# The seven-product down matmul in tile 1 as well, its weight sums made during tile 0, and one copy moved to ScalarE in the last two tiles

## The chip, the core and the metric

The kernel runs on one core of a Trainium2 chip. The core has a matrix engine (TensorE, "PE" in the profile), a vector engine (VectorE, "DVE"), a scalar engine (ScalarE, "ACT"), GpSimd ("POOL") and SyncE ("SP"), which here only starts transfers. Each engine works through its own queue strictly in order; between engines there are only semaphores. The metric is the time on the device in microseconds, median of several executions.

## The reference

Two stages follow each other. The first is attention over pooled keys: `k` and `v` (batch 8, heads 8, sequence 576, head size 64) are averaged over groups of 8 tokens, which leaves 72 keys for each head; `q` attends to these with a softmax. The second is a feed-forward layer over the 4608 tokens of 512 features that result:

```python
k_p = k.reshape(B, H, Sp, pool, D).mean(axis=3)
v_p = v.reshape(B, H, Sp, pool, D).mean(axis=3)
scores = scale * np.matmul(q, k_p.transpose(0, 1, 3, 2))
attn = softmax(scores)
x = concat_heads(np.matmul(attn, v_p))
h = x @ w_in                        # 4608x512 @ 512x2048
g = h * np.cos(h)
out = g @ w_out                     # 4608x2048 @ 2048x512
```

## The kernel before

The 4608 tokens are nine tiles of 512, numbered t = 0 to 8; the eight batches of 576 tokens are numbered b. While the feed-forward layer of tile t runs, the attention of batch t + 1 is woven between its matmuls. The order of instructions is written out by hand: each engine's queue holds its instructions in the order in which the program text issues them.

**A tile.** The up part computes `h` in eight pairs of 128 features, 64 matmuls of 512 columns in all (`up_mm`). A pair is written to one of four places in PSUM: `banks[0]` to `banks[2]`, each two banks wide, or the two `obanks`. `up_bank` gives the rotation, and from tile `FIRST` on it is banks 0, 2, 1, obanks, 0, 2, 1, 0. For each pair ScalarE makes the cosine (as a sine with a shifted argument) and VectorE multiplies it with the PSUM values into `g_sb` (`up_g`). A place can be written again only when that multiplication has read it. The down part multiplies `g` with `w_out`. Its outputs are in the `obanks` and leave through VectorE copies and SP transfers.

**Two forms of the down part.** Tiles below `FIRST` (0 and 1 before the change) use the plain one: 64 matmuls of 512 columns, with the attention's steps inserted at given positions of the loop by a list `fill`. Tiles from `FIRST` on use `down_products`: the 2x2 blocks of `g` (features by tokens) and of `w_out` are combined as in Winograd's form of Strassen's method, which needs seven products of blocks in place of eight: 7 x 16 matmuls of 256 columns. For this it needs sums of blocks:

- of the weights, once: `w2`, `w3`, `w4`, made by `put_weights`, and the second column block of the first two weight tiles, replaced in place by a difference in `put_first_weights`. Each has two halves i = 0, 1. `put_weights(0)` is done by GpSimd at the end of tile 0's program text; `put_weights(1)` by VectorE during tile 1's up part; `put_first_weights` by VectorE after tile 1's down part. Each is one operation of 128x1024 bf16, with both inputs in SBUF.
- of `g`, in every tile: `put_g12` (two operations), `put_g3` and `put_g4`, by VectorE, for the first half after the fourth, fifth and sixth up pair, and for the second half after the first products.

The results of the seven products lie in two PSUM places, called A and Bb, and are read out between products by the list `reads`. The first read copies the first product to `p1_sb` by VectorE (`each`, with no other operand). The third product overwrites A and so must wait for that copy. In tiles 1 to 6 attention steps lie between the products (scores after the first, values of one unit after the second, third and fourth); tile 7 has only the rest of the last batch; tile 8 has none, and there A and Bb are spread over separate banks (`apart`).

**Around the change.** GpSimd starts the loads of `k`, `q`, `v` for the batch after next, then (in tile 0) makes `put_weights(0)`, and then pools `k` and `v` by additions (`pool_add`, lines 151 to 159). SP's queue holds the output transfers and the two transposes (`q_transpose`, `k_transpose`), issued during the up part of tiles 1 to 6. At the end of tile 0's down part VectorE has, in this order, the multiplications of the values of batch 1 and the copies of the last two output blocks.

Of the kernel before, what the change touches and what calls it, by code (L numbers as in the profile page):

```python
# [20 lines left out]
def kernel(  # L21
# [9 lines left out]
    nc = tc.nc  # L31
# [11 lines left out]


    ORDER = (0, 2, 4, 6, 1, 3, 5, 7, 8)
    FIRST = 2

    SEG = ((0, 256), (256, 256), (512, 64))
    REST = (SEG[2], (0, H))
# [324 lines left out]
    def down_products(t):  # L374

        def of(w, m=0):
            return lambda fc: w[fc // 4][:, fc % 4, m * HM:(m + 1) * HM]

        def part(x):
            return lambda fc, p: x[:, fc, p * 128:(p + 1) * 128]  # L380

        apart = t == NT - 1
        if apart:
            A, Bb = [[x[:, 0:HM] for x in two] for two in (obanks, (banks[1][:, 0, :], banks[2][:, 0, :]))]
        else:
            A, Bb = [[obanks[i][:, p * HM:(p + 1) * HM] for p in range(2)] for i in (1, 0)]
        products = [
            (A, True, part(g_part(0, 0, 0, HF)), of(w_out_sb[0:2])),
            (Bb, True, part(g_part(1, 0, 0, HF)), of(w_out_sb[2:4])),
            (A, True, part(g2), of(w2)),  # L390
            (Bb, True, part(g1), of(w_out_sb[0:2], 1)),
            (A, False, part(g3), of(w3)),
            (Bb, False, part(g4), of(w_out_sb[2:4], 1)),
            (A, False, part(g_part(1, 1, 0, HF)), of(w4)),
        ]
        mms = []
        for n, (bank, first, g, w) in enumerate(products):
            order = [(fc, p) for fc in range(HF) for p in range(2)]
            if apart and n == 6:
                order.sort(key=lambda x: x[1])  # L400
            for fc, p in order:
                mms.append(lambda bank=bank, first=first, g=g, w=w, fc=fc, p=p: nc.tensor.matmul(  # L402
                    bank[p], lhsT=g(fc, p), rhs=w(fc),
                    start=(first and fc == 0 and (apart or p == 0)), stop=(fc == HF - 1 and (apart or p == 1)),
                    skip_group_check=not first))

        p1, v16, q15 = [msb.tile([128, 2, HM], FP32, name=n, tag=n, bufs=1) for n in ("p1_sb", "v_sb", "q_sb")]
        o1, o2 = [msb.tile([128, 2, d_model], FP32, name="o_two", tag="o_two", bufs=3) for _ in range(2)]
        m1, m2 = slice(0, HM), slice(HM, d_model)

        def each(out, bank, other=None, m=slice(0, HM), tk=None):

            for p in range(2) if apart else (slice(0, 2),):
                ps = bank[p] if apart else obanks[1 if bank is A else 0].rearrange("p (a m) -> p a m", a=2)
                if other is None:
                    nc.vector.tensor_copy(out=out[:, p, m], in_=ps)  # L416
                else:
                    nc.vector.tensor_tensor(out=out[:, p, m], in0=ps, in1=other[:, p], op=ADD)  # L418
                if apart and tk is not None:
                    rows_out(t, tk, out, (p,), m, (nc.sync, nc.scalar))  # L420

        reads = [
            lambda: each(p1, A),
            lambda: each(o1, Bb, p1, m1, 0),
            lambda: each(v16, A, p1),
            lambda: each(q15, Bb, p1),
            lambda: each(o2, A, q15, m2, 1),
            lambda: (each(o1, Bb, v16, m2, 0), apart or rows_out(t, 0, o1)),
            lambda: (each(o2, A, p1, m1, 1), apart or rows_out(t, 1, o2)),
        ]  # L430
        return [mms[i * 2 * HF:(i + 1) * 2 * HF] for i in range(7)], reads
# [99 lines left out]
    for t in range(NT):  # L531
# [5 lines left out]
        for n, fp in enumerate(up_order(t)):  # L537
            up_mm(t, fp, 2 if n < 2 else 0)
            between = ()
            if t == 0:  # L540
                if fp == 4:
                    puts = pool_k_mm(1, obanks[0], 0, 2), pool_k_mm(1, obanks[1], 2, 4)
                elif fp in (5, 6):
                    g0 = 9 * (fp - 5)
                    puts = q_transpose_mm(1, obanks[0], g0, g0 + 5), q_transpose_mm(1, obanks[1], g0 + 5, g0 + 9)
                if fp in (4, 5, 6):
                    puts[0](vec)
                    between = ((puts[1], act),)
            up_g(t, fp, between)
            if t >= FIRST and 3 <= n < 6:  # L550
                (put_g12, put_g3, put_g4)[n - 3](0)
            if t == 1 and 3 <= n < 6:
                put_weights(1, nc.vector, n - 3)
            if 0 < t and b < B:
                if n == 0:
                    q_transpose(b)
                elif n == 2:
                    k_transpose(b)
# [18 lines left out]
        if t == 0:  # L577
            fill[1:] = [(2, S_(0, 0)), (8, lambda: pool_v_mm(1, banks[1])), (8, lambda: values(t, REST, banks[2])),
                        (11, S_(1, 0)), (13, V_(0, 1)), (18, S_(2, 2)), (21, V_(1, 0, later)), (26, S_(3, 1)),
                        (32, lambda: later.pop()()), (32, V_(2, 2)), (40, V_(3, 0))]  # L580
        elif t < FIRST:
            us = BY_TOKENS

            def scores_of(*parts):

                def go():
                    for f in scores_mm, scores_exp:
                        for b_, u, bank in parts:
                            f(b_, u, banks[bank])
                return go  # L590

            fill = [(4, scores_of((b, us[0], 2), (b, us[1], 0))), (14, V_(0, 1, later)), (16, lambda: later.pop()()),
                    (19, V_(1, 2)), (35, scores_of((b, us[2], 0), (b, us[3], 1), (t, REST, 2))),
                    (38, V_(2, 0)), (43, lambda: values(t, REST, banks[1])), (46, V_(3, 2))]
        if t < FIRST:
            fi = 0
            for n, (ms, fc) in enumerate(mms):
                while fi < len(fill) and fill[fi][0] <= n:
                    fill[fi][1]()
                    fi += 1  # L600
                down_mm(obanks[ms % 2], ms, fc)
                if fc == FFCH - 1:
                    down_out(t, ms, obanks[ms % 2])
            if t + 1 == FIRST:
                for i in range(2):
                    put_first_weights(i)
        else:
            products, reads = down_products(t)

            def product(i, j=0, k=2 * HF):  # L610
                for mm in products[i][j:k]:
                    mm()

            us = BY_TOKENS
            later = []

            u0, u1, u2, u3 = [(b, us[i], banks[j]) for i, j in enumerate((2, 1, 0, 1))]
            ur = (t, REST, banks[2])

            def scores_of(*parts):  # L620
                for part in parts:
                    scores_mm(*part)
                for part in parts:
                    scores_exp(*part)

            def muls():
                while later:
                    later.pop(0)()

            steady, rest = b < B, t < B  # L630
            if rest:
                exp_tables()
            product(0)
            if steady:
                scores_of(u0, u1, u2)
            elif rest:
                scores_of(ur)
            product(1)
            put_g12(1)
            reads[0]()  # L640
            put_g3(1)
            reads[1]()
            put_g4(1)
            if steady:
                values(*u0, later)
            product(2)
            reads[2]()
            muls()
            if steady:
                values(*u1, later)  # L650
            product(3)
            reads[3]()
            muls()
            if steady:
                values(*u2, later)
            product(4)
            reads[4]()
            muls()
            if steady:
                scores_of(ur, u3)  # L660
            product(5, 0, 4)
            if rest:
                values(*ur, later)
            product(5, 4, 12)
            muls()
            if steady:
                values(*u3, later)
            product(5, 12)
            reads[5]()
            muls()  # L670
            product(6)
            reads[6]()
# [5 lines left out]
        if b + 1 < B:  # L678
# [2 lines left out]
            load_kv(b + 1, "v", v)  # L681
            if t == 0:
                put_weights(0, nc.gpsimd)
            pool_add(b + 1, "k")
            pool_add(b + 1, "v")
# [28 lines left out]
```

The softmax here doesn't subtract the row's maximum and nothing guards it: scores larger than these inputs give would overflow.

## Time and profile before

| what | us |
|---|---|
| median of 5 runs | 295.24 (294.73 to 296.24) |
| the profiled execution, its own time | 296.24 |
| its span, from the first to the last instruction | 294.5 |
| TensorE busy | 282.1 (96%) |
| VectorE busy | 225.5 (77%) |
| ScalarE busy | 206.8 (70%) |
| GpSimd busy | 147.5 (50%) |
| tile 0, from its first up matmul to tile 1's | 17.42 to 53.53 |
| tile 1 | 53.53 to 85.64: 32.11 |
| tile 2 | 85.64 to 115.96: 30.32 |
| tile 3 | 115.96 to 145.89: 29.93 |
| tile 7 | 235.69 to 263.15: 27.46 |
| tile 8, to the end of the span | 263.15 to 294.5 |

The time of an execution is a little longer than its span. "Busy" is the time covered by an engine's instructions; the ends of matmuls are modelled and overlap with the next one, so the start times of matmuls tell more than their durations. In lines of the order of time the first number is the start, the second the time from the start of the first to the end of the last instruction of the group, and the brackets hold the idle time before it and what ended that. A line of the busy time by stage holds the stage, its length, the busy time of PE, PEld, DVE, ACT and POOL with the number of instructions, the granted clock, the share of the transfer engines and GB/s.

### The profile page before, as it was taken

To read this page: it belongs to the slowest core of one execution; us is meant where nothing else is said; L and a number is where in the kernel's file an instruction comes from. 1 tells how busy PE (TensorE), PEld (TensorE's weight loads), DVE (VectorE), ACT (ScalarE), POOL (GpSimd) and SP (SyncE) were. 2 spreads that over 40 slices of the span, in tenths; PEclk is the share of its full clock that TensorE was granted. 3 is DMA by queue.
4 is the path that set the end of the run, shared out by engine and by line. 5 is a ranking of instruction groups with operands and counts; after the bars stand their busy time and mean duration, and the time that the engine had idled before them with its cause. 6 is when DMAs were issued, how large, how long until landed. Compare 5 with 4: busy or idle time off the path is not lost. (4 is left out here: it accounts for less than half of the span.)

```text
span 294.5 us, 5317 instructions
## 1 busy us (share of the span) xinstructions
PE 282.1 (96%) x2096; PEld 173.4 (59%) x2120; DVE 225.5 (77%) x306; ACT 206.8 (70%) x261; POOL 147.5 (50%) x144
## 2 busy tenths in 40 slices
PE   7889999999999999999999999999999999999984
PEld 2545544444544587458745874588458844774673
DVE  5458637486479998799879887997798879846972
ACT  3786898368777789679967997699769976336500
POOL 8453059993996399636984499349900000000000
PEclk9999999999999999999999999999999999999998
DMA  7999999557908790969195929691840060005014
GB/s 155 196 207 206 207 205 204 111 97 102 196 17 174 96 147 22 203 89 162 24 179 89 173 42 196 91 176 27 173 73 2 4 143 0 2 21 122 2 36 107
DMA packets 44488, 32.95 MB, mean 112 GB/s; under 512 B 22192, under 2 KB 40112, under 8 KB 44464
## 3 DMA queue, kind: packets, MB, share of 16 engines
q0 software_dynamic: 19744, 18.07, 39.4%
q1 hardware_dynamic: 24080, 14.03, 22.4%
q10 hardware_dynamic: 640, 0.52, 0.7%
q8 instruction: 16, 0.26, 0.4%
q14 instruction: 8, 0.07, 0.1%
HBM read 36.70 MB, written 9.44 MB: 157 GB/s over the span
## 5 line engine op out<-in xcount | busy, mean ns | idle before, releaser
L317 PE MATMUL bank<-xT,w_in_sb 128*128 128x512 bf16 x503 | 114.8, 379 | 1.1
L327 ACT ACTIVATE cos<-bank,half_pi 128x1024 f32<-128x1024 f32 x65 | 71.5, 1114 | 47.8 <-PE bank L317 45.6
L317 PEld LDWEIGHTS <-w_in_sb 128*128 128x128 bf16 x576 | 56.0, 98 | 66.7 <-issue 0.9
L331 DVE TENSOR_TENSOR g_sb<-bank,cos 128x1024 bf16<-128x1024 f32 x65 | 78.3, 1218 | 22.1 <-ACT cos L327 22.0
L151 POOL TENSOR_TENSOR half_sums<-kv_st 72x512 f32<-72x512 bf16 x48 | 55.7, 1188 | 28.3 <-DMA kv_st<-in_k_dram 27.9
L262 DVE TENSOR_TENSOR xT<-bank,inv 64x512 bf16<-64x512 f32 (+1 forms) x72 | 45.3, 630 | 18.6 <-ACT inv L258 17.6
L257 ACT ACTIVATE inv<-bank 64x512 f32<-64x512 f32 (+1 forms) x72 | 39.2, 544 | 12.4 <-PE bank L251 11.4
L402 PEld LDWEIGHTS <-g 128*128 128x128 bf16 x448 | 42.9, 98 | 7.9 <-issue 3.0
L229 ACT ACTIVATE ex<-bank 72x1024 bf16<-72x1024 f32 (+1 forms) x40 | 35.0, 929 | 3.2 <-PE bank L222 3.1
L402 PEld LDWEIGHTS <-g_sb 128*128 128x128 bf16 x336 | 32.1, 98 | 6.8 <-issue 1.0
L153 POOL TENSOR_TENSOR half_sums<-half_sums 72x512 f32<-72x512 f32 x24 | 30.9, 1306 | 0.0
L334 PE MATMUL obank<-w_out_sb,g_sb 128*128 128x512 bf16 x123 | 29.9, 379 | 0.7 <-DMA w_out_sb<-in_moe_w_out_dram 0.3
L402 PE MATMUL obank<-w,g 128*128 128x256 bf16 x224 | 26.9, 272 | 1.5 <-DVE p_sb L416 1.4
L402 PE MATMUL obank<-w_out_sb,g_sb 128*128 128x256 bf16 x208 | 25.1, 273 | 0.2 <-DVE g_sb L331 0.2
L402 PE MATMUL obank<-w_out_sb,g 128*128 128x256 bf16 x192 | 24.8, 273 | 0.0
L258 ACT ACTIVATE inv<-inv 128x512 f32<-128x512 f32 (+1 forms) x36 | 21.0, 583 | 1.1
L251 PE MATMUL bank<-ex,vz 72*128 72x256 bf16 (+1 forms) x176 | 20.0, 243 | 0.0
L334 PEld LDWEIGHTS <-g_sb 128*128 128x128 bf16 x128 | 11.9, 98 | 12.9 <-issue 1.4
L251 PEld LDWEIGHTS <-vz 72*128 72x128 bf16 x176 | 13.7, 97 | 4.5 <-DVE xT L262 0.5
L156 POOL TENSOR_TENSOR kp<-half_sums 72x512 bf16<-72x512 f32 x12 | 15.0, 1266 | 0.5
L222 PE MATMUL bank<-qT,kk 64*72 64x256 bf16 (+1 forms) x192 | 13.3, 251 | 1.3 <-DVE g_sb L331 1.0
L402 PE MATMUL obank<-w,g_sb 128*128 128x256 bf16 x112 | 13.4, 273 | 0.0
(83 smaller groups left out, 251.1 us busy)
## 6 DMA issues: line engine op xcount, KB each, us to landing
out_dram<-o_two SPq DMA_DIRECT2D x64, 128.0 KB, 2.4
kv_st<-in_v_dram POOLq DMA_DIRECT2D x8, 576.0 KB, 13.3
kv_st<-in_k_dram POOLq DMA_DIRECT2D x7, 576.0 KB, 8.0
q_b<-in_q_dram POOLq DMA_DIRECT2D x6, 576.0 KB, 10.2
w_in_sb<-in_moe_w_in_dram POOLq DMA_DIRECT2D x4, 512.0 KB, 14.4
w_out_sb<-in_moe_w_out_dram POOLq DMA_DIRECT2D x4, 512.0 KB, 18.3
q_b<-in_q_dram POOLq DMA_DIRECT2D x4, 288.0 KB, 12.9
g_sb<-in_k_dram SPq DMA_DIRECT2D x1, 576.0 KB, 3.7
```

What stands on the lines that cost most here:

```text
L151: add(out=s[:, h:h + 2], in0=x[:, h:h + 2, 0:4, :], in1=x[:, h:h + 2, 4:8, :], op=ADD)
L153: add(out=s[:, h:h + 4, 0:2, :], in0=s[:, h:h + 4, 0:2, :], in1=s[:, h:h + 4, 2:4, :], op=ADD)
L229: nc.scalar.activation(out=ex[:, 0:nh * n].rearrange("p (a n) -> p a n", a=2), in_=pair[:Sp, :, 0:nh * n // 2], func=ACTF.Exp, scale=scale ...
L251: nc.tensor.matmul(pair[:, hp, (i // 2) * n:(i // 2 + 1) * n], lhsT=vz[b % 2][:, pj, 2 * hp:2 * hp + 2, :].rearrange("p a d -> p (a d)"), ...
L257: nc.scalar.activation(out=inv[half[1 - hp]], in_=pair[half[1 - hp], hp, 0:w], func=ACTF.Ln)
L258: nc.scalar.activation(out=inv, in_=inv, func=ACTF.Exp, scale=-1.0)
L262: nc.vector.tensor_mul(out=x_out(b, u, half[hp]), in0=cols(pair[half[hp], hp, :], u), in1=cols(inv[half[1 - hp]], u))
L317: nc.tensor.matmul(h[j] if h is obanks else h[:, j, :], lhsT=w_in_sb[fc // 4][:, ki, (fc % 4) * 128:(fc % 4 + 1) * 128], rhs=xT[:, ki, t * ...
L327: nc.scalar.activation(out=c, in_=ps, func=ACTF.Sin, bias=half_pi[:, :1])
L331: nc.vector.tensor_mul(out=o, in0=ps, in1=c)
L334: nc.tensor.matmul(o, lhsT=g_sb[:, fc, ms * 128:(ms + 1) * 128], rhs=w_out_sb[fc // 4][:, fc % 4, :], start=(fc == 0), stop=(fc == FFCH - 1))
L402: mms.append(lambda bank=bank, first=first, g=g, w=w, fc=fc, p=p: nc.tensor.matmul(bank[p], lhsT=g(fc, p), rhs=w(fc), start=(first and fc ...
```

## The change

`FIRST` becomes 1, so tile 1 uses the seven-product form and the four-place rotation. The branch of the loop that held the plain form for tile 1 is removed. The weight sums are moved into tile 0: `put_weights(1)` into its down part, after the matmuls numbered 36, 38 and 46, and `put_first_weights` after the issue of `put_weights(0)` at its end. The first product's copy is done by ScalarE in the last two tiles (7 and 8).

```diff
-    FIRST = 2
+    FIRST = 1
...
                 if other is None:
-                    nc.vector.tensor_copy(out=out[:, p, m], in_=ps)
+                    (nc.scalar.copy if t >= B - 1 else nc.vector.tensor_copy)(out=out[:, p, m], in_=ps)
...
             if t >= FIRST and 3 <= n < 6:
                 (put_g12, put_g3, put_g4)[n - 3](0)
-            if t == 1 and 3 <= n < 6:
-                put_weights(1, nc.vector, n - 3)
...
-        elif t < FIRST:
-            us = BY_TOKENS
...
-            fill = [(4, scores_of((b, us[0], 2), (b, us[1], 0))), (14, V_(0, 1, later)), (16, lambda: later.pop()()),
-                    (19, V_(1, 2)), (35, scores_of((b, us[2], 0), (b, us[3], 1), (t, REST, 2))),
-                    (38, V_(2, 0)), (43, lambda: values(t, REST, banks[1])), (46, V_(3, 2))]
         if t < FIRST:
...
                 down_mm(obanks[ms % 2], ms, fc)
                 if fc == FFCH - 1:
                     down_out(t, ms, obanks[ms % 2])
-            if t + 1 == FIRST:
-                for i in range(2):
-                    put_first_weights(i)
+                if n in (36, 38, 46):
+                    put_weights(1, nc.vector, (36, 38, 46).index(n))
...
             if t == 0:
                 put_weights(0, nc.gpsimd)
+                for i in range(2):
+                    put_first_weights(i)
             pool_add(b + 1, "k")
```

More of the change, by code (lines that the diff above doesn't have):

```diff
@@ L580 @@
                         (32, lambda: later.pop()()), (32, V_(2, 2)), (40, V_(3, 0))]
-        elif t < FIRST:
-            us = BY_TOKENS
[L584 to L590, printed above, removed]
-            fill = [(4, scores_of((b, us[0], 2), (b, us[1], 0))), (14, V_(0, 1, later)), (16, lambda: later.pop()()),
-                    (19, V_(1, 2)), (35, scores_of((b, us[2], 0), (b, us[3], 1), (t, REST, 2))),
-                    (38, V_(2, 0)), (43, lambda: values(t, REST, banks[1])), (46, V_(3, 2))]
         if t < FIRST:
```

## The prediction, made before the changed kernel was run

> **What bounds the kernel now.** First the page's busy shares, then a table by stage, cut where each tile's up matmuls begin on TensorE (tile 1 at 53.53, tile 2 at 85.64, tile 3 at 115.96; the last row is tile 6).
>
> ```profile
> PE 282.1 (96%) x2096; PEld 173.4 (59%) x2120; DVE 225.5 (77%) x306; ACT 206.8 (70%) x261; POOL 147.5 (50%) x144
> ```
>
> ```profile
> 53.53:85.64 32.11, 31.36 (x174) 15.16 (x176) 19.64 (x24) 23.22 (x30) 26.51 (x24) 1.00 0.64 113
> 85.64:115.96 30.32, 29.98 (x223) 19.55 (x224) 28.76 (x37) 23.68 (x31) 21.92 (x20) 1.00 0.62 102
> 115.96:145.89 29.93, 29.67 (x224) 19.68 (x224) 26.17 (x34) 24.30 (x32) 19.71 (x19) 1.00 0.71 121
> 205.76:235.69 29.93, 29.66 (x224) 19.70 (x224) 25.57 (x34) 24.31 (x32) 7.57 (x7) 1.00 0.30 62
> ```
>
> TensorE has no holes worth the name: a seven-product tile takes 29.93 us every time, tile 1 (plain down matmul) takes 32.11 and tile 2 30.32. So time goes only where TensorE issues less, or where it is made to wait. In a steady tile the 64 up matmuls take 13.82 us, or 0.216 each.
>
> Next, the order of time on VectorE around the end of tile 0, and on GpSimd in the same stretch (columns: start, duration of the group, instruction).
>
> ```profile
> 48.06 1.39 DVE L262 TENSOR_TENSOR xT<-bank,inv 64x512 bf16<-64x512 f32 x2 [0.21 <-ACT inv L258]
> 50.44 1.39 DVE L262 TENSOR_TENSOR xT<-bank,inv 64x512 bf16<-64x512 f32 x2 [0.99 <-ACT inv L258]
> 52.87 0.69 DVE L339 COPY o_two<-obank 128x512 f32<-128x512 f32 x1 [1.04 <-PE obank L334]
> 53.73 0.69 DVE L339 COPY o_two<-obank 128x512 f32<-128x512 f32 x1 [0.17 <-PE obank L334]
> 57.47 2.36 DVE L331 TENSOR_TENSOR g_sb<-bank,cos 128x1024 bf16<-128x1024 f32 x2 [3.04 <-ACT cos L327]
> ...
> 62.96 1.76 DVE L351 TENSOR_TENSOR w<-w_out_sb,w_out_sb 128x1024 bf16<-128x1024 bf16 x1
> ...
> 87.93 2.51 DVE L355 TENSOR_TENSOR w_out_sb<-w_out_sb 128x1024 bf16<-128x1024 bf16 x2
> ```
>
> ```profile
> 47.65 4.48 POOL L151 TENSOR_TENSOR half_sums<-kv_st 72x512 f32<-72x512 bf16 x4 [0.34 <-DMA kv_st<-in_k_dram]
> 52.09 2.49 POOL L153 TENSOR_TENSOR half_sums<-half_sums 72x512 f32<-72x512 f32 x2
> ...
> 61.67 2.50 POOL L153 TENSOR_TENSOR half_sums<-half_sums 72x512 f32<-72x512 f32 x2
> 64.25 1.60 POOL L159 TENSOR_TENSOR vz<-half_sums 72x512 bf16<-72x512 f32 x1
> ...
> 88.17 3.40 POOL L153 TENSOR_TENSOR half_sums<-half_sums 72x512 f32<-72x512 f32 x2
> ```
>
> VectorE has idle stretches of 1.0 and 3.0 us there, where the moved weight sums go. But GpSimd works without a pause from 47.65 to 65.8, and the last rows show what that does: a 128x1024 bf16 sum takes 0.68 us alone (65.78 and 67.51), 1.76 at 62.96, and 2.51 for the pair at 87.93. GpSimd pays too: 3.40 for two operations of 1.26.
>
> Last, TensorE's only repeated wait of size.
>
> ```profile
> 254.18 1.91 PE L402 MATMUL obank<-w,g 128*128 128x256 bf16 x16 [0.66 <-DVE p_sb L416]
> ...
> 281.38 2.13 PE L402 MATMUL obank<-w,g 128*128 128x256 bf16 x16 [0.76 <-DVE p_sb L416]
> ```
>
> In tiles 7 and 8 the third product waits for the first product's copy: no attention work stands between them to cover it.
>
> **What the Trainium skill says.** "SBUF — State Buffer", section "Who interferes with whom": a VectorE instruction with two SBUF inputs and a GpSimd instruction that reads SBUF share one read interface; whichever comes second is blocked until the first ends; with one SBUF input VectorE is free of it. The trace agrees to a tenth: GpSimd's operation before 88.17 ends at 88.21, the first sum of the pair runs from 88.08 to 88.76, GpSimd's next then ends 0.45 late at 89.89, the second sum runs 89.76 to 90.44, and GpSimd's last ends at 91.57. So: a sum starts 0.13 before the end of the GpSimd operation that holds the interface, and GpSimd starts 0.14 before the end of the sum; they alternate. The multiplications of a PSUM bank (1.14 us from start to start when back to back) never stretch. "ScalarE: Activation LUTs", section "Table sets: the hidden batching unit": copy is in every table set. The trace agrees: copies at 8.31 and 30.42, under different sets, have no table load beside them.
>
> **Part 1, tile 1's down matmul.** It removes 64 matmuls of 512 columns and issues 112 of 256 in seven products. The price is what tiles 3 to 6 take: 29.93 against 32.11, so -2.18 us if nothing disturbs it. Scores, values, the transposes issued by SP and the four g sums per half come with it and are inside the 29.93.
>
> **Part 2, tile 2.** It loses the late start of VectorE (copies of the plain tile, then the pair at 87.93): 30.32 becomes 29.93, -0.39.
>
> **Part 3, the moved sums.** Five sums now stand in VectorE's queue of tile 0: three before, between and after the last multiplications of values, two after the output copies. Then tile 1 has g1 and g2 after its fourth multiplication. I place each by the alternation above, with GpSimd's operations 1.15 us (sums of the staged data) or 1.26.
> - w3 arrives at 49.40 and gets the interface at 49.78; done 50.46. w2 follows behind GpSimd: 51.34 to 52.02.
> - The last values multiplication, ready at 50.44, runs 51.96 to 53.35 (before: ended 51.83). It frees bank 0, which tile 1's first up matmul needs at 53.53: 0.13 us to spare, so nothing. Its xT columns are needed only after eight matmuls.
> - w4: 54.12 to 54.80. Output copies end at 55.43 and 56.04 (before 54.42), so SP's two transposes behind their stores go 1.6 later: the second from 60.4 to 62.0, landed near 66, asked for at 71: hidden.
> - First in-place sum: it arrives at 55.95, GpSimd's next operation at 56.00. I take VectorE as first: 55.95 to 56.63. The second: 57.62 to 58.30.
> - Multiplications of tile 1 then start at 58.22 instead of 57.47; the fourth ends at 63.02.
> - g1 arrives at 63.05, runs 63.83 to 64.52; g2 waits again, 65.51 to 66.20. The fifth multiplication ends at 67.34.
> - The eighth up pair reuses bank 0 and is due at 53.53 + 56 x 0.216 = 65.61. It goes at 67.39: **1.78 us lost**. (In tile 3 the fifth multiplication ended at 127.50 for a pair due at 128.04: 0.54 to spare.)
> - g3 and g4 arrive at 67.3 and 69.0, when GpSimd's chain is at its end (69.1): no wait. The first product's fc 6 then waits 0.44, but the scores' known wait of 0.16 shrinks: net 0.35 more than in a steady tile.
>
> Stall in tile 1: 1.78 + 0.35 = 2.13, which eats nearly all of part 1: tile 1 takes 29.93 + 2.13 = 32.06, that is -0.05. GpSimd's loads for batch 3 leave 2.9 us later (69.3 for 66.4), its chain ends at 94.9 and tile 2's g1 arrives at 94.5: 0.2 of wait, within the 0.54. After that GpSimd's idle time at its gate (14.0 us over four tiles) takes the delay up.
>
> **Part 4, the copy on ScalarE.** Tile 7: ScalarE is free from 252.73 (exp of 0.59) to 260.29; a copy of 128x512 from PSUM is near 0.60 (the Ln of that shape was 0.59), ready at 253.4. The third product could go at 251.60 + 16 x 0.109 = 253.35 and went at 254.18: -0.75. Tile 8: ScalarE idles after 278.28; two copies of 128x256 at about 0.42 (what an Exp of that shape takes) are done by 279.7, before the second product ends at 280.45. The product after it began at 283.34 and can begin at 282.20: -1.14, less some 0.06 for the second bank's reading. g2 ends at 280.99, before its second half is asked for at 281.3. Together -1.83.
>
> Sum: -0.05 - 0.39 - 1.83 = -2.27. The profiled execution took 296.24 (span 294.5, 1.74 around it) and would become 293.97 with a span of 292.2; the change is the same on the median: 295.24 - 2.27 = **293.0**.
>
> **Rivals.**
> - *GpSimd first.* The first in-place sum loses the race of 0.05 us at 56.0. Then it and all behind it come 1.07 later: stall 3.2, tile 1 +1.02, in all -1.2: 294.0. For it: the margin is below what I can place. Against: only that the placing gives VectorE the lead.
> - *No contention.* The sums fit into the idle 1.0 and 3.0 us: -2.18 - 0.39 - 1.83 = -4.4: 290.8. Against it: every sum measured beside a reading GpSimd stretched.
> - *The copy gains nothing*, since g2 or the reading of the second bank holds the third product: -0.44 alone: 294.8. Against: both were placed above, with 0.1 to 0.3 us to spare.
> - *Slower.* The interface is lost at g3 and g4 too, and at the first in-place sum. Each costs 1.07: 2.13 + 3 x 1.07 = 5.3 of stall, 0.9 above the 4.40 that all gains make together: 296.1. It decides from a GpSimd chain that ends about 1.3 us later than 69.1. For it: each of my sums pushes that chain. Against: I counted these pushes.
>
> **How the numbers follow.** Chances: forecast 0.48, GpSimd first 0.25, no contention 0.08, copy without gain 0.10, slower 0.09. The range 291.9 to 294.9 holds the first, second and fourth, leaving 0.17 out. A measurement of this kernel can tell about 0.3% (0.9 us). Faster: 0.48 + 0.08 + most of GpSimd first (0.21) = 0.77; same: the rest of it and the copy without gain, 0.14; slower 0.09.
>
> **What would show it.** Right: tile 1 still near 32 us from up start to up start, with g1 and g2 of its first half near 1.5 us each and a hole before its last up pair; tile 2 at 29.9; no wait before the third product of tiles 7 and 8. Wrong: the five sums at 0.68 each (then near 290.8), the first multiplication of tile 1 after 59 (then 294), a table load beside the copy, or a hole at the start of tile 1, where bank 0 has only 0.13 us.

## The result, and the profile after

The changed kernel takes as long as the kernel before: 295.37 us (median of 43 executions, 293.73 to 298.95) against 295.46 (80 executions, 294.51 to 297.32). The ratio is 0.9996, with a 95% interval of 0.9985 to 1.0008. The forecast was 293.0, with 291.9 to 294.9 as its range: it was wrong by 2.4 us. The two ends of the range of executions have moved apart, which matters below.

The profiled execution took 296.21 with a span of 294.4 (before: 296.24 and 294.5). From up start to up start, where "due" is the end of the tile ahead:

| stage | before | after | difference |
|---|---|---|---|
| up to tile 1 (when its first matmul is due) | 53.53 | 53.34 | -0.2 |
| tile 1 | 32.11 | 34.59 | +2.5 |
| tile 2 | 30.32 | 29.93 | -0.4 |
| tile 7 | 27.46 | 26.64 | -0.8 |
| tile 8 to the end of the span | 31.35 | 30.17 | -1.2 |

So all that was gained elsewhere is lost in tile 1. The order of time on TensorE through tile 1 of the changed kernel (start, duration of the group, instruction, and in brackets the idle time before it):

```profile
53.77 5.35 PE L317 MATMUL bank<-xT,w_in_sb 128*128 128x512 bf16 x24 [0.43 <-DVE xT L262]
...
60.85 5.34 PE L317 MATMUL bank<-xT,w_in_sb 128*128 128x512 bf16 x24
68.77 2.42 PE L317 MATMUL bank<-xT,w_in_sb 128*128 128x512 bf16 x8 [2.57 <-DVE g_sb L331]
70.98 3.10 PE L402 MATMUL obank<-w_out_sb,g_sb 128*128 128x256 bf16 x16
74.00 0.84 PE L222 MATMUL bank<-qT,kk 64*72 64x256 bf16 x12
```

There is the hole ahead of the last up pair that was forecast, but longer: the pair was due at 53.77 + 56 x 0.2158 = 65.85 and went at 68.77, 2.92 late. Ahead of the tile there is a small hole of 0.43, which the forecast had put at nothing. And the pair itself takes 2.21 from start to next start, where eight such matmuls take 1.73, and the first product 3.02 to the scores, where a steady tile takes 1.84. The busy time by stage tells most of why (stage, its length, busy time of PE, PEld, DVE, ACT, POOL with counts, then the granted TensorE clock, the transfer share and GB/s):

```profile
53.77:65.85 12.08, 12.03 (x55) 5.43 (x57) 11.90 (x11) 6.73 (x7) 11.85 (x10) 1.00 0.55 108
65.85:68.77 2.92, 0.35 (x3) 0.07 (x2) 2.89 (x4) 0.00 (x0) 2.92 (x4) 1.00 0.00 0
68.77:70.98 2.21, 2.21 (x9) 0.87 (x9) 2.21 (x4) 1.11 (x1) 1.27 (x2) 0.77 0.62 63
70.98:74.00 3.02, 3.02 (x17) 2.05 (x15) 2.80 (x4) 2.40 (x2) 0.00 (x0) 0.60 1.11 158
```

After the hole the granted clock is 0.77 and then 0.60. These are averages of two values, as a finer cut of the same 5.2 us shows: full clock for 1.21 us, half clock for 3.41 us, full clock again.

```profile
68.77:69.98 1.21, 1.21 (x6) 0.58 (x6) 1.21 (x2) 1.11 (x1) 1.21 (x2) 1.00 0.47 30
69.98:73.39 3.41, 3.41 (x16) 1.98 (x14) 3.22 (x4) 2.15 (x2) 0.06 (x1) 0.50 1.03 148
73.39:74.00 0.61, 0.61 (x6) 0.37 (x4) 0.58 (x2) 0.24 (x1) 0.00 (x0) 1.00 1.08 120
```

Tile 1's loss against a steady tile is then 0.43 + 2.92 + 0.48 + 1.18, less 0.34 by which the later scores wait less: 4.67, and 29.93 + 4.67 = 34.60. Not all of the 1.18 is the clock's: about 0.44 of it is a wait for VectorE that was forecast, as the run with the hole filled shows below.

VectorE in the same stretch, to be set beside the rows before the change:

```profile
49.14 1.60 DVE L351 TENSOR_TENSOR w<-w_out_sb,w_out_sb 128x1024 bf16<-128x1024 bf16 x1
50.77 1.52 DVE L351 TENSOR_TENSOR w<-w,w_out_sb 128x1024 bf16<-128x1024 bf16 x1
52.33 1.39 DVE L262 TENSOR_TENSOR xT<-bank,inv 64x512 bf16<-64x512 f32 x2
53.75 1.44 DVE L351 TENSOR_TENSOR w<-w_out_sb,w 128x1024 bf16<-128x1024 bf16 x1
55.22 1.29 DVE L339 COPY o_two<-obank 128x512 f32<-128x512 f32 x2
56.43 3.24 DVE L355 TENSOR_TENSOR w_out_sb<-w_out_sb 128x1024 bf16<-128x1024 bf16 x2
59.59 3.68 DVE L331 TENSOR_TENSOR g_sb<-bank,cos 128x1024 bf16<-128x1024 f32 x3
63.18 1.28 DVE L331 TENSOR_TENSOR g_sb<-obank,cos 128x512 bf16<-128x512 f32 x2
64.50 1.42 DVE L363 TENSOR_TENSOR g<-g_sb 128x1024 bf16<-128x1024 bf16 x1
65.94 1.64 DVE L364 TENSOR_TENSOR g<-g,g_sb 128x1024 bf16<-128x1024 bf16 x1
67.50 1.21 DVE L331 TENSOR_TENSOR g_sb<-bank,cos 128x1024 bf16<-128x1024 f32 x1
```

Every one of the seven sums in this stretch takes about twice its 0.68 us or more. VectorE has no idle time left from 49.1 to the fifth multiplication at 67.5, whose end at 68.71 releases the last up pair. The time lost stands in the durations of these sums, not in a wait that the profile names.

In the last two tiles the third product no longer waits:

```profile
255.26 1.91 PE L402 MATMUL obank<-w,g 128*128 128x256 bf16 x16
...
281.54 1.91 PE L402 MATMUL obank<-w,g 128*128 128x256 bf16 x16
```

Before they began 2.58 and 2.67 us after the start of the product ahead of them, now 1.76 and 1.75.

The lower clock isn't in every execution. Each has a mean granted clock for its whole span, and 3.41 us at half clock lower the mean of a span of 294.4 by 0.006. One execution, of 298.95 at a clock of 0.983, was in a slower state that the kernel before shows too, and is left out here; of the 43 others, the profiled one among them, 23 have a mean of 0.988 to 0.994 and a median time of 296.16, and 20 have 0.998 or more and a median of 294.57. Of the kernel before, 54 of 56 executions that have a clock on record (in the experiments below) have 0.997 or more. That the medians of the two kernels agree is an accident: it needs about half of the executions on each side.

### The profile page after: what moved, and what is told of

It reads as the page before. It is cut to its first block, busy times and chain, and to the rows that moved or that the text cites. A ratio compares the mean times of both kernels' runs of the same rounds, so it can differ in the third digit from the quotient of the medians.

```text
span 294.4 us, 5421 instructions
## 1 busy us (share of the span) xinstructions
PE 281.1 (95%) x2146; PEld 178.5 (61%) x2168; DVE 236.1 (80%) x315; ACT 207.9 (71%) x265; POOL 148.8 (51%) x144
## 4 chain that ended last, share of the span: by engine, by line
PE 84%; DVE 6%; ACT 4%; issue 2%; DMA 2%; POOL 0%; POOLq 0%; DVEq 0%; ACTq 0%
PE bank L317 36%; PE obank L402 29%; PE bank L251 5%; PE obank L317 5%; DVE g_sb L331 3%; PE bank L222 3%; PE obank L334 2%; ACT cos L327 2%; DMA q_b<-in_q_dram 2%; PE bank L402 2%; ACT ex L229 1%; DVE xT L262 1%; DVE w L351 1%; DVE g L364 1%; DVE g L363 0%
## 5 line engine op out<-in xcount | busy, mean ns | idle before, releaser
L151 POOL TENSOR_TENSOR half_sums<-kv_st 72x512 f32<-72x512 bf16 x48 | 57.5, 1226 | 27.3 <-DMA kv_st<-in_k_dram 26.9
L402 PEld LDWEIGHTS <-g 128*128 128x128 bf16 x512 | 49.0, 98 | 6.8 <-issue 1.2
L402 PEld LDWEIGHTS <-g_sb 128*128 128x128 bf16 x384 | 37.5, 99 | 8.2 <-issue 1.7
L402 PE MATMUL obank<-w,g 128*128 128x256 bf16 x256 | 30.6, 272 | 0.0
L402 PE MATMUL obank<-w_out_sb,g_sb 128*128 128x256 bf16 x240 | 29.9, 280 | 0.0
L402 PE MATMUL obank<-w_out_sb,g 128*128 128x256 bf16 x224 | 29.0, 273 | 0.0
L402 PE MATMUL obank<-w,g_sb 128*128 128x256 bf16 x128 | 15.3, 273 | 0.0
L317 PE MATMUL obank<-xT,w_in_sb 128*128 128x512 bf16 x63 | 15.1, 379 | 0.1
L334 PE MATMUL obank<-w_out_sb,g_sb 128*128 128x512 bf16 x61 | 15.0, 380 | 0.1
```

The costliest lines, as they stand in the source:

```text
L151: add(out=s[:, h:h + 2], in0=x[:, h:h + 2, 0:4, :], in1=x[:, h:h + 2, 4:8, :], op=ADD)
L317: nc.tensor.matmul(h[j] if h is obanks else h[:, j, :], lhsT=w_in_sb[fc // 4][:, ki, (fc % 4) * 128:(fc % 4 + 1) * 128], rhs=xT[:, ki, t * ...
```

## The experiments

Differences to the changed kernel are taken from its median of 295.37, though the runs come from several sessions; the kernel before had 295.16 to 295.46 in each of these, so a few tenths mean nothing.

Theory: the copy on ScalarE brings 2.0 us. Tile 1 loses what that and tile 2 bring, because the sums moved beside GpSimd's pooling wait for the interface that the two engines share; and the hole that this makes in TensorE's work costs a second time, by the clock. Rivals: the two parts are each neutral; VectorE simply has too much to do in tile 1, whatever GpSimd does; the lower clock has another cause.

**The copy alone.** The kernel before, with one line of the change:

```diff
-                    nc.vector.tensor_copy(out=out[:, p, m], in_=ps)
+                    (nc.scalar.copy if t >= B - 1 else nc.vector.tensor_copy)(out=out[:, p, m], in_=ps)
```

> The kernel before with the copy of the first product on ScalarE in tiles 7 and 8 as its only edit. Theory (the two parts of the change have opposite signs): tile 7 goes from 27.46 to 26.6 and tile 8 loses 1.2 as in the changed kernel, so the whole time falls by 2.0 us, to 293.5. Rival (the copy only moves the wait, and tile 1 is neutral): 295.4.

Measured: 293.38, ratio 0.9934 (0.9920 to 0.9949): -1.9 us. The copy is worth what was expected of it.

**The change without the copy.** The same line back on VectorE in the changed kernel.

> The changed kernel with the copy back on VectorE in all tiles. Theory: tile 1 stays at 34 to 35 us, against 32.1 in the kernel before, tile 2 gives 0.4 back, and nothing pays for the rest: slower than the kernel before by 1.5 to 2 us, 297.3. Rival (tile 1 neutral): 295.4.

Measured: 297.42, ratio 1.0077 (1.0058 to 1.0097): +2.1 us. The two parts have opposite signs and nearly one size, which settles the first rival. The hole is there without the copy too, as TensorE's order of time shows, and with it 3.41 us at half clock; five of the six executions have a mean clock of 0.991 to 0.994.

```profile
67.67 3.49 PE L317 MATMUL bank<-xT,w_in_sb 128*128 128x512 bf16 x8 [2.47 <-DVE g_sb L331]
```

```profile
67.53:70.94 3.41, 3.27 (x8) 1.17 (x8) 3.41 (x5) 1.11 (x1) 3.14 (x5) 0.50 0.20 19
```

**The hole filled.** TensorE gets idle work where it had waited:

```diff
+            if t == 1 and n == 7:
+                for _ in range(12):
+                    nc.tensor.matmul(obanks[0], lhsT=w_in_sb[0][:, 0, 0:128], rhs=w_in_sb[0][:, 0, :])
             up_mm(t, fp, 2 if n < 2 else 0)
```

> The changed kernel with twelve idle matmuls (128x512, into an output place that is not in use then) ahead of the last up pair of tile 1, where TensorE had waited 2.9 us. The work that TensorE waits for comes no earlier. Theory A (the wait costs twice, since the clock that TensorE is granted falls after it): the granted clock stays at 1.00 behind the pair and the tile is shorter by about 1.3 us, 294.1. Theory B (the lower clock has another cause, or costs nothing): the same time as the changed kernel, 295.4, or more by what the idle matmuls take beyond the wait, and the lower clock is still there.

Measured: 294.66 over 22 executions, ratio to the kernel before 0.9981 (0.9969 to 0.9993). That is 0.7 below the changed kernel, not 1.3; but every one of the 22 executions has a mean granted clock of 0.997 or more, and 294.66 is within 0.1 of the median of those executions of the changed kernel that kept their clock (294.57). So the filling does what Theory A says, and only for the half of the executions that had lost it; the expected size took one profiled execution for all of them. The means are 295.50 (43 executions) and 294.76 (22); spread over the 23 alone, the difference of 0.74 is an estimated 1.4 us each. The busy time by stage of this kernel, over the idle matmuls, and over the pair that follows with most of the first product:

```profile
65.00:68.12 3.12, 3.12 (x16) 1.37 (x14) 3.08 (x4) 0.13 (x1) 3.04 (x3) 1.00 0.00 0
68.12:71.00 2.88, 2.88 (x20) 1.82 (x19) 2.88 (x4) 2.07 (x2) 2.88 (x4) 1.00 0.15 10
```

The order of time on TensorE behind the pair:

```profile
69.85 1.47 PE L402 MATMUL obank<-w_out_sb,g_sb 128*128 128x256 bf16 x12
71.59 0.61 PE L402 MATMUL obank<-w_out_sb,g_sb 128*128 128x256 bf16 x4 [0.27 <-DVE g_sb L331]
72.13 0.99 PE L222 MATMUL bank<-qT,kk 64*72 64x256 bf16 x12
```

At full clock the first product still takes 2.28 to the scores, 0.44 more than in a steady tile, because its last four matmuls wait for a multiplication on VectorE. Set against this run, the clock took 2.21 - 1.73 = 0.48 from the pair and 3.02 - 2.28 = 0.74 from the first product of the changed kernel's profiled execution; the later scores gave 0.15 of that back, which leaves an estimate of about 1.1 us.

**GpSimd without the pooling of batch 2.** This kernel leaves out work, and the outputs of batch 2 are not those of the reference; it only serves to keep GpSimd quiet.

```diff
-            pool_add(b + 1, "k")
-            pool_add(b + 1, "v")
+            if t > 0:
+                pool_add(b + 1, "k")
+                pool_add(b + 1, "v")
```

> The changed kernel without GpSimd's pooling of k and v of batch 2, so that GpSimd does nothing between 47 and 65 us; the outputs of batch 2 are then not those of the reference. Theory (the sums are long because GpSimd holds the shared interface): each moved sum takes 0.68 us, tile 1 takes 29.9 to 30.1 us, and the time is 4.6 us below the changed kernel, 290.8. Rival (VectorE has too much to do in tile 1 whatever GpSimd does): the five sums and g1, g2 add 0.68 each, tile 1 stays over 33, and the time over 294.

Measured: 292.99, ratio 0.9909 (0.9891 to 0.9927): -2.4 against the changed kernel, half of what was expected. Its profiled execution (296.02, its slowest) shows a fault of the experiment: with nobody reading the staged tiles, the load of v started 8 us later, and behind it GpSimd's own weight sums 6.5 us later (46.6 to 53.5). They now met VectorE's first two sums, which took 2.64 and 2.49. The sums after 53.5 took 0.69 and the pair 1.28. It also shows the clock once more: a hole of 2.43 at the start of the tile, and then this stage of 24 matmuls, which take 5.18 at the full clock, with 3.41 us at half clock in it:

```profile
55.52:62.39 6.87, 6.87 (x24) 2.79 (x25) 4.39 (x7) 2.12 (x2) 0.00 (x0) 0.75 0.54 115
56.03:59.44 3.41, 3.41 (x10) 1.24 (x9) 2.64 (x5) 0.00 (x0) 0.00 (x0) 0.50 0.31 69
```

The other six executions have 292.03 to 294.11 and a mean clock of 0.997 or more.

So it was made again with one element of each staged tile read (the outputs of batch 2 are still not those of the reference):

```diff
+            for which in "kv":
+                if t > 0:
+                    pool_add(b + 1, which)
+                else:
+                    nc.gpsimd.tensor_copy(out=gate, in_=staged.pop((which, b + 1))[0:1, 0, 0, 0:1])
```

> As the run without GpSimd's pooling of batch 2, but GpSimd reads one element of each of the two staged tiles in its place, so that its weight sums and its loads should keep their time; the outputs of batch 2 are not those of the reference. Theory (the shared interface): GpSimd's own weight sums end near 46.7 as in the changed kernel, all five moved sums and g1, g2 take 0.68 to 0.69 us, no hole in tile 1, tile 1 29.9 to 30.1 us, 290.8. Rival (too much work on VectorE in tile 1 in any case): tile 1 over 31 us, 292.5 or more.

Measured: 291.06, ratio 0.9865 (0.9842 to 0.9889): -4.3 against the changed kernel. GpSimd's weight sums end at 45.97, and VectorE's order of time and the stage of tile 1 read:

```profile
48.08 0.69 DVE L351 TENSOR_TENSOR w<-w_out_sb,w_out_sb 128x1024 bf16<-128x1024 bf16 x1
48.80 0.69 DVE L351 TENSOR_TENSOR w<-w,w_out_sb 128x1024 bf16<-128x1024 bf16 x1
...
52.94 1.28 DVE L355 TENSOR_TENSOR w_out_sb<-w_out_sb 128x1024 bf16<-128x1024 bf16 x2
...
61.11 0.69 DVE L363 TENSOR_TENSOR g<-g_sb 128x1024 bf16<-128x1024 bf16 x1
61.83 0.69 DVE L364 TENSOR_TENSOR g<-g,g_sb 128x1024 bf16<-128x1024 bf16 x1
```

```profile
52.13:82.06 29.93, 29.72 (x225) 19.68 (x225) 26.27 (x35) 22.77 (x30) 15.63 (x15) 1.00 0.63 105
```

The same instructions stand in VectorE's queue, and tile 1 takes exactly what a steady tile takes. VectorE's work fits; only the waiting for GpSimd doesn't, and the second rival is settled. The loss in tile 1 is contention and what follows from it.

**The sums of g later in tile 1.** If the sums can't be kept from GpSimd, those that delay the fifth multiplication can stand behind it:

```diff
-            if t >= FIRST and 3 <= n < 6:
+            if t == 1 and n == 5:
+                put_g12(0)
+            elif t > 1 and 3 <= n < 6:
                 (put_g12, put_g3, put_g4)[n - 3](0)
...
+            if t == 1:
+                put_g3(0)
             put_g3(1)
...
+            if t == 1:
+                put_g4(0)
             put_g4(1)
```

> The changed kernel with the first half's sums of g in tile 1 issued later: g1 and g2 after the sixth multiplication in place of the fourth, g3 and g4 in the down part beside those of the second half. Nothing is left out. Theory (the time goes in the hole before the last up pair, which waits for the fifth multiplication behind g1 and g2): the fifth multiplication ends near 65.7, the hole is below 0.3 us, the granted clock stays at 1.00, tile 1 takes about 31 us and the time is 3.7 us below the changed kernel's slower runs, 291.8. Rival (VectorE's backlog only moves on to the first product): tile 1 stays over 32.5, 294.

Measured: 293.28 (ratio 0.9929, 0.9907 to 0.9951): -2.1 against the changed kernel, short of the expected 291.8. The hole before the last up pair is gone, every execution keeps a clock of 0.997 or more, and tile 1 takes 31.73 (expected about 31; the rival said over 32.5). Most of the rest moved further on, as the rival said, though it is smaller: four sums, with one read of a product between them, now stand ahead of the multiplications of the second unit of values, and the scores of the fourth unit wait for these:

```profile
81.08 0.41 PE L222 MATMUL bank<-qT,kk 64*72 64x256 bf16 x4 [1.10 <-DVE xT L262]
```

A hole of 1.10 is not followed by a lower clock.

**And w2 behind the last values multiplication.** The positions 36, 38, 46 become 36, 41, 46.

> As the run before it, and the second of the three weight sums in tile 0's down part (w2) is issued after the last values multiplication in place of ahead of it. Theory (the small hole at the start of tile 1 is bank 0 held by that multiplication): the wait of 0.4 us at the start of tile 1 is gone and the time falls by another 0.4 us, 291.4. Rival (VectorE is behind all the same, and the up pairs feel it later): no difference.

Measured: 293.48 (ratio 0.9943, 0.9921 to 0.9965): no difference. The wait at the start of tile 1 is gone, and one of 0.37 stands before the fifth up pair: the rival was right. VectorE's backlog stays nearly the same: the fifth multiplication of the tile starts at 64.78, against 64.84 without this move.

**g4 of the second half later still.** The edit is against the run with the later sums.

```diff
             if t == 1:
                 put_g4(0)
-            put_g4(1)
+            else:
+                put_g4(1)
...
             reads[3]()
             muls()
+            if t == 1:
+                put_g4(1)
```

> As the run with the later sums of g, with one more move in tile 1: the second half's g4 after the second unit's multiplications, in place of beside the first half's g4. Theory (in that run the scores of the fourth unit waited 1.1 us for the second unit's multiplications, which stood behind four sums of g in a row): this hole closes, tile 1 goes from 31.7 to about 30.7 us and the time falls by 1.0 us against that run. Rival (the hole only moves on to the sixth product, which then waits for g4): no gain.

> The kernel before with the copy on ScalarE in the last two tiles alone, once more beside the run above. Theory: 293.4 as in the first run of it, and about 1 us above the run beside it, since tile 1 in the seven-product form then gains about 1 us on the plain form. Rival: the two are equal within 0.3 us, and the seven-product form in tile 1 is worth nothing even when its sums are placed better.

Measured in one session: 292.65 (ratio 0.9907, 0.9883 to 0.9931) and, for the copy alone, 293.31 (0.9937, 0.9916 to 0.9958). The hole of 1.10 is closed and tile 1 takes 30.82, but tile 2 takes 30.30 instead of 29.93, since its first matmuls wait for the last multiplications of values. So 0.6 us are gained against the run with the later sums, which is not clear of noise (another session, and the intervals overlap), and 0.7 against the copy alone beside it, where about 1.0 was expected of each. Of the six executions here only one (293.09) reaches the range of the copy alone (293.04 to 295.10), so the 0.7 stands. The seven-product form in tile 1 is worth this much with its sums placed this way; this version is faster than both kernels compared here.

## Why the prediction was wrong, point by point

- **The lock and its rule** (section "Who interferes with whom" of the Trainium skill's page "SBUF — State Buffer") were right: the moved sums took 0.69 with GpSimd quiet and 1.4 to 1.7 beside its pooling. So was the sum over the four parts: with GpSimd out of the way tile 1 took 29.93 and the time was 291.06, where the rival without contention had 290.8.
- **The copy on ScalarE**: forecast -1.83, measured -1.9. A copy of 128x512 took 0.57 and the two of 128x256 0.65 together. No table load was added for them (18 before and after), as the Trainium skill's page "ScalarE: Activation LUTs", section "Table sets: the hidden batching unit", lets one expect.
- **Tile 2**: forecast -0.39, measured 30.32 to 29.93.
- **The first step that failed** is the line "I take VectorE as first", the first in-place sum at 55.95 against GpSimd at 56.00. GpSimd was first:

```profile
56.28 1.27 POOL L156 TENSOR_TENSOR kp<-half_sums 72x512 bf16<-72x512 f32 x1
56.43 1.67 DVE L355 TENSOR_TENSOR w_out_sb<-w_out_sb 128x1024 bf16<-128x1024 bf16 x1
```

The pair ended at 59.67, not 58.30, and this 1.37 is what the fifth multiplication ended later than forecast (68.71, not 67.34). In all six profiles with these sums beside the pooling the pair took 3.2 to 3.5 us, which is the rival "GpSimd first". The placing took the start of GpSimd's chain from one execution (47.65); in the changed kernel's it began at 46.81, 0.84 earlier against 0.3 for VectorE, so VectorE's first sum met another operation and waited 0.9 instead of 0.4. A lead of 0.05 us cannot be carried through a chain of operations whose phase moves by 0.5.

- **"0.13 us to spare, so nothing"** failed for the same reason: the last values multiplication ended at 53.72, not 53.35, and tile 1 began 0.43 late.
- **The hole**: forecast 1.78, measured 2.92. This 1.14 and the 0.43 make 1.57 of the 2.53 us by which tile 1 was longer than forecast (34.59 against 32.06).
- **The 0.44 of wait in the first product** was right, as the filled run shows.
- **The second step that failed** is a term put at nothing: forecast and rivals all price what TensorE does after the hole at its full clock, without giving a reason. In 23 of 43 executions it was granted half of it for a while, and they took 296.16 against 294.57. In the profiled execution this cost about 1.1 us; the estimate from the filled run is 1.4 in each of the 23. The rest of the 1.6 stays open; longer holes may be those that lose the clock.

The first failure alone would have left the result inside the range: 294.57 where the clock was kept, close to the 294.0 of "GpSimd first". The second carried the median out of it, to 295.4. The prediction had named two of the signs that came, a hole at the start of tile 1 and its first multiplication after 59 (it was at 59.59).

The range failed because no outcome let a longer hole cost anything beyond its own length. The chance of a stall larger than forecast was put at 0.34 with the slower case, too low for a race without a margin.

## What to carry to other kernels

Before work is moved into another engine's idle time, look at what shares its path: VectorE sums with both inputs in SBUF cost 0.68 us where GpSimd was quiet, mostly 1.3 to 1.8 beside its pooling (operations of 1.15 to 1.26) and up to 2.64 beside its own weight sums (2.12 each), so "idle" has to mean idle on both. Where the sum of delays reaches an engine that was never idle, its hole can be followed by slower work; here a filled hole kept the clock in every execution. And where a forecast hangs on an order that a tenth of a microsecond decides, take the worse order.

## What the runs showed of the hardware that was not expected

- Three profiles have a hole of 2.43 to 2.57 us (idle time) in an otherwise full TensorE: the changed kernel, the one without the copy, and the first run without pooling. In each the granted clock was 0.50 for 3.41 us, once, and 1.00 before and after. In this order, the half clock began 1.2 us after the end of the hole, 0.1 before it and 0.5 after it. Holes of 1.10 (in two profiles) and one of 1.68 (while the run with the later sums started up) were not followed by it, and no other profile here has it while TensorE has work.
- In the changed kernel 23 of 43 executions have the lower mean clock, without the copy 5 of 6, without pooling at first 1 of 7. Which executions it strikes, and whether the others had a shorter hole, isn't settled, since only one of each has a trace.
- Twelve matmuls whose results nobody reads, in place of the hole, kept the mean clock at 0.997 or more in 22 of 22 executions.
- Taking away the only reader of a staged tile moved a load that it seemed not to touch by 8 us (37.9 to 45.8), with the weight sums behind it; one element read was enough to bring it back (36.8).
